# Two chains of the experts' second products as the halves of one PSUM bank

## Chip, cores and metric

One Trainium2 chip, one of its cores. The metric is the device time of one execution, in microseconds, as the median of several runs. TensorE (PE) multiplies and writes PSUM, which has 8 banks of 512 fp32 columns in each of 128 partitions; VectorE (DVE) and ScalarE (ACT) read PSUM; GpSimd (POOL) works from SBUF; SyncE (SP) issues the DMAs.

## What is computed

Linear attention with a random-feature map (4 batches, 8 heads, 576 tokens), whose output is the 2304 x 512 input of a mixture of eight experts. The change lies in the experts' part:

```
def _moe_ref(x, w_gate, w1, w2):
    N, D = x.shape                        # 2304, 512
    E = w_gate.shape[1]                   # 8
    logits = x @ w_gate
    P = np.exp(logits - logits.max())
    for _ in range(8):
        P /= P.sum(1, keepdims=True) + 1e-09
        P /= P.sum(0, keepdims=True) + 1e-09
        P *= N / E
    out = np.zeros((N, D))
    for e in range(E):
        h = np.maximum(x @ w1[e], 0.0)    # w1[e]: 512 x 1024
        out += P[:, e:e + 1] * (h @ w2[e])
    return out
```

## The kernel before

The attention takes the first 180 us or so. Then each of the two products of an expert is done as a 2 x 2 block product by a scheme of seven block products, M1 to M7, in the order 1, 5, 6, 3, 7, 2, 4 (`ORDER`), in which running sums in PSUM serve several blocks of the result. Each factor is split in a high and a low part (`wh`, `wl`; for the left operands `ah`/`al`, `sh`/`sl`, `sh2`/`sl2`, `bh`/`bl`), and each block product is six matmuls: high by high, low by high, high by low, for two halves of the inner dimension.

A unit is an expert and half of its inner columns: 16 units. The 18 row tiles of the tokens go in pairs, a tile t0 of the upper and one, t1, of the lower half of a chunk: nine pairs a unit, and 16 x 9 = 144 steps in all (s = 0 to 143). `second(s, i)` does block product i of the second product of a step, with six matmuls of 256 columns (line 751). Between them the main loop places the pieces of the first product of later steps (`first`, six matmuls of 384 columns each, line 650, into tiles hx and hz of other banks).

The four banks of pool `ps4` hold the sums of `second`. M1, M6, M7, M4 are summed in tile x, one onto the other; M5 and M3 in tile z; M2 alone in tile w. After each of the seven an output operation adds the sum so far, weighted by the gate's column, to one quarter of the pair's result (tiles `out`, 128 x 512 each, one for t0 and one for t1): line 777, a VectorE operation of 256 columns with PSUM and SBUF as sources. For expert 0 (18 steps) the weight comes later and the operation is an addition (line 769) or, for a first value, a ScalarE copy (767). In the last three steps those of M1 and M6 go over ScalarE and GpSimd (774, 775). Since x and z go on summing, M6 waits for M1's operation, M7 for M6's, M4 for M7's and M3 for M5's.

The left operands are made by ScalarE and VectorE: ah and al for M1, sh and sl for M7 and M5 (lines 699 to 713), sh2 and sl2 for M6 and M3, bh and bl for M2 and M4 (lines 725 to 730). bh and bl have one buffer each: those of the next step are written when M4 of this step has read them. GpSimd makes block sums of weights now and then (line 216) and, in the last three steps, sl and sl2.

The order on each engine is not written out by hand in this part: a scheduler orders the instructions by a model of their times and by what depends on what, and gives each tile of a pool a bank that is free then. So a change in one place moves instructions in many.

The lines that set chain and quarter are:

```
key, start = {1: ("x", 1), 6: ("x", 0), 7: ("x", 0), 4: ("x", 0), 5: ("z", 1), 3: ("z", 0), 2: ("w", 1)}[i]
if start:
    acc[key] = bank(key)
pb = acc[key][:, :HD]                     # HD = 256
r, col, init = {
    1: (0, 0, 1), 6: (0, 1, 1), 7: (1, 1, 0), 4: (1, 0, 1), 5: (1, 1, 1), 3: (0, 1, 0), 2: (0, 0, 0),
}[i]                                      # which tile of the pair, which half
```

The two that the change joins are M3, right half of t0, and M2, left half of t0.

Of the kernel before, what the change touches and what calls it, by code (L numbers as in the profile page):

```python
# [22 lines left out]
def moe_attention_kernel(  # L23
# [44 lines left out]
    HD = DM // 2  # L68
# [11 lines left out]
    def bank(name):  # L80
        return ps[0].tile([P, 512], F32, tag="b", name=name)
# [515 lines left out]
    outt = {}  # L597
# [3 lines left out]
    def order(u):  # L601

        return [NCH - 1] + list(range(NCH - 1)) if u == 0 else list(range(NCH))
# [69 lines left out]
    def tiles_of(u, n):  # L673

        c, j = order(u)[n // (CT // 2)], n % (CT // 2)
        return [CT * c + j, CT * c + j + CT // 2]
# [58 lines left out]
    acc = {}  # L735

    def second(s, i):


        u, n = steps[s]  # L740
        key, start = {1: ("x", 1), 6: ("x", 0), 7: ("x", 0), 4: ("x", 0), 5: ("z", 1), 3: ("z", 0), 2: ("w", 1)}[i]
        final = s == len(steps) - 1
        if final and i == 4:

            key, start = "y", 1
        if start:
            acc[key] = bank(key)
        pb = acc[key][:, :HD]
        prods = [(a, b, f) for a, b in ((0, 0), (0, 1), (1, 0)) for f in range(2)]
        for j, (a, b, f) in enumerate(prods):  # L750
            nc.tensor.matmul(  # L751
                pb, lhsT=ops[s][i][a][:, f], rhs=wt[u, 2, i][b][:, f],
                start=bool(start) and j == 0, stop=j == len(prods) - 1, skip_group_check=True,
            )
        e, fb = units[u]
        r, col, init = {
            1: (0, 0, 1), 6: (0, 1, 1), 7: (1, 1, 0), 4: (1, 0, 1), 5: (1, 1, 1), 3: (0, 1, 0), 2: (0, 0, 0),
        }[i]
        pair = tiles_of(u, n)
        t = pair[r]  # L760
        if u == 0 and i == 1:
            for tt in pair:
                outt[tt] = op_.tile([P, DM], F32, name=f"out{tt}")
        o = outt[t][:, col * HD : (col + 1) * HD]
        if e == 0:
            if u == 0 and init:
                nc.scalar.copy(o, pb)  # L767
            else:
                nc.vector.tensor_tensor(o, pb, o, op=ALU.add)
            return  # L770
        p = prob[:, t, e : e + 1]
        if s >= len(steps) - CT // 2 and i in (1, 6):
            sp = op_.tile([P, HD], F32, tag="sp", bufs=2, name="sp")
            nc.scalar.mul(sp, pb, p)
            nc.gpsimd.tensor_tensor(o, sp, o, op=ALU.add)
        else:
            nc.vector.scalar_tensor_tensor(o, in0=pb, scalar=p, in1=o, op0=ALU.mult, op1=ALU.add)  # L777
        if final and i == 7:
            o = outt[t][:, :HD]
            nc.vector.scalar_tensor_tensor(o, in0=pb, scalar=p, in1=o, op0=ALU.mult, op1=ALU.add)  # L780
# [163 lines left out]
    for s, (u, n) in enumerate(steps):  # L944
# [12 lines left out]
        for k, i in enumerate(ORDER):  # L957
            second(s, i)
            if more and (n, k) in W2AT:
                split(u + 1, 2, ORDER[W2AT.index((n, k))])  # L960
            if k < ((5, 5, 4) if s > 2 else (3, 4, 3))[n % 3] and todo:
                pc = todo.pop(0)
                first(*pc)
                j = ORDER.index(pc[2])
                if pc[1] == order(pc[0])[-1] and pc[3] == 1 and pc[0] + 1 < len(units) and j + 1 < len(ORDER):
                    split(pc[0] + 1, 1, ORDER[j + 1])
            if i == 7 and s + 1 < len(steps):
                left_operands_a(s + 1)
            if k in (1, 4):
                next(gate, None)  # L970
# [38 lines left out]
```

## Time and profile before

| | us |
|---|---|
| median of three runs (lowest, highest) | 1613.99 (1610.22, 1614.95) |
| the profiled execution | 1611.28 |
| its span | 1609.4 |
| PE busy | 1574.7 (98%) |
| weight loads of PE (PEld) busy | 1543.1 (96%) |
| DVE busy | 1388.4 (86%) |
| ACT busy | 774.8 (48%) |
| POOL busy | 298.1 (19%) |

An engine's busy time is the union of its instructions' times. A matmul of 256 columns stands in the trace with 0.28 us, but the next starts after half of that, so a pause of PE shorter than the overlap does not show as idle time; its weight loads, which the profile lists apart, show it sooner. A wait is put down to the engine whose signal came last. "x2" on a line of the timeline means two instructions in a row, and its time is that from the first one's start to the last one's end.

### The profile page before, as it was taken

What the parts mean: (1) busy time and instruction counts of PE and PEld (TensorE: products, weight loads), DVE (VectorE), ACT (ScalarE), POOL (GpSimd) and SP (SyncE); (2) the same over time, 40 slices, a digit from 0 to 9 for tenths busy, and PEclk for the clock granted to TensorE, in tenths of its full rate; (3) what the DMA queues carried; (4) which work ended last, traced back from release to release, by engine and by line L of the source; (5) the groups of instructions that cost most, each with busy time, mean ns of one, the idle gap of its engine ahead of it and who ended that gap; (6) DMA issues with size and microseconds to landing.
All of it is one profiled execution on the core that took longest, in us unless ns stands there. A gap on an engine that the chain in (4) does not pass through costs nothing.

```text
span 1609.4 us, 31434 instructions
## 1 busy us (share of the span) xinstructions
PE 1574.7 (98%) x12318; PEld 1543.1 (96%) x12318; DVE 1388.4 (86%) x2721; ACT 774.8 (48%) x1396; POOL 298.1 (19%) x304
## 2 busy tenths in 40 slices
PE   7998899999999999999999999999999999999998
PEld 6877899999999999999999999999999999999997
DVE  5998798999888987989898988889898889889777
ACT  7987565444344444434354444444443444444333
POOL 6664321101021111101021111112010111110003
PEclk9999999999999999999999999999999999999999
DMA  8646865666665665656656665746565566655552
GB/s 205 153 146 240 305 229 203 212 209 208 220 217 192 233 211 171 224 197 215 206 206 213 211 220 181 253 170 223 203 208 210 211 216 212 212 189 198 193 197 79
DMA packets 105314, 329.79 MB, mean 205 GB/s; under 512 B 14800, under 2 KB 43984, under 8 KB 105168
## 3 DMA queue, kind: packets, MB, share of 16 engines
q1 hardware_dynamic: 105168, 327.79, 60.2%
q8 instruction: 98, 1.61, 0.4%
q14 instruction: 48, 0.39, 0.1%
HBM read 306.53 MB, written 21.23 MB: 204 GB/s over the span
## 4 chain that ended last, share of the span: by engine, by line
PE 86%; DVE 10%; ACT 2%; POOL 1%; issue 1%; DMA 0%; SPq 0%; DVEq 0%; ACTq 0%
PE hx L650 24%; PE x L751 23%; PE hz L650 18%; PE z L751 12%; PE w L751 6%; DVE sm L687 2%; DVE out L777 2%; PE pp L389 1%; DVE bl L687 1%; DVE sqs L399 1%; DVE wl L247 1%; POOL sq L353 1%; DVE sl L726 1%; PE tp L374 1%; DVE xs L123 1%
## 5 line engine op out<-in xcount | busy, mean ns | idle before, releaser
L650 PE MATMUL hx<-xs,wh 128*128 128x384 f32 x1536 | 372.2, 336 | 2.7 <-ACT out L767 1.2
L777 DVE SCALAR_TENSOR_TENSOR out<-x,prob,out 128x256 f32<-128x256 f32 x497 | 234.2, 477 | 59.5 <-PE x L751 57.8
L650 PE MATMUL hz<-xs,wh 128*128 128x384 f32 x1152 | 281.7, 337 | 0.0
L650 PEld LDWEIGHTS hx<-xs,wh 128*128 128x128 f32 x1536 | 268.6, 188 | 4.3 <-ACT xs L119 2.0
L216 POOL TENSOR_TENSOR st<-st 128x512 f32<-128x512 f32 x79 | 126.3, 1598 | 702.6 <-DVE wl L247 698.1
L650 PEld LDWEIGHTS hz<-xs,wh 128*128 128x128 f32 x1152 | 203.2, 189 | 0.7 <-ACT xs L119 0.4
L650 PE MATMUL hx<-xs,wl 128*128 128x384 f32 x768 | 198.7, 335 | 0.0
L729 ACT ACTIVATE bh<-hr 128x512 fp32r<-128x512 f32 x144 | 91.2, 633 | 211.6 <-PE x L751 206.9
L777 DVE SCALAR_TENSOR_TENSOR out<-z,prob,out 128x256 f32<-128x256 f32 x252 | 120.3, 478 | 56.5 <-PE z L751 55.9
L725 ACT CAST sh<-sm 128x512 fp32r<-128x512 f32 x144 | 89.6, 622 | 152.7 <-PE z L751 106.1
L246 ACT CAST wh<-st 128x512 fp32r<-128x512 f32 x172 | 102.9, 620 | 104.6 <-PE hx L650 43.9
L650 PE MATMUL hz<-xs,wl 128*128 128x384 f32 x576 | 151.7, 336 | 0.0
L687 DVE SCALAR_TENSOR_TENSOR sm<-hr,sm 128x256 f32<-128x256 f32 x288 | 137.1, 476 | 2.6
L650 PEld LDWEIGHTS hx<-xs,wl 128*128 128x128 f32 x768 | 138.4, 188 | 0.0
L247 DVE TENSOR_TENSOR wl<-st,wh 128x512 fp32r<-128x512 f32 x169 | 121.8, 730 | 12.0 <-ACT wh L246 11.5
L687 DVE SCALAR_TENSOR_TENSOR bl<-hr,bh 128x512 fp32r<-128x512 f32 x144 | 119.5, 830 | 0.1
L751 PE MATMUL x<-wh,sh 128*128 128x256 f32 x576 | 116.9, 283 | 2.6 <-DVE out L777 1.6
L751 PE MATMUL x<-wl,sh 128*128 128x256 f32 x576 | 118.2, 282 | 0.7 <-DVE wl L247 0.7
L751 PE MATMUL x<-wh,sl 128*128 128x256 f32 x576 | 117.2, 282 | 0.0
L751 PE MATMUL z<-wl,sh 128*128 128x256 f32 x576 | 117.2, 281 | 0.0
L751 PE MATMUL z<-wh,sl 128*128 128x256 f32 x576 | 115.3, 282 | 1.7 <-DVE sl L709 1.7
L751 PE MATMUL z<-wh,sh 128*128 128x256 f32 x576 | 116.6, 281 | 0.2 <-DVE out L777 0.2
(161 smaller groups left out, 3410.5 us busy)
## 6 DMA issues: line engine op xcount, KB each, us to landing
xs<-xd SPq DMA_DIRECT2D x329, 768.0 KB, 4.4
st<-in_moe_w_dram SPq DMA_DIRECT2D x64, 512.0 KB, 5.1
xd<-xs SPq DMA_DIRECT2D x21, 768.0 KB, 4.3
k<-in_k_dram SPq DMA_DIRECT2D x8, 512.0 KB, 7.1
v<-in_v_dram SPq DMA_DIRECT2D x8, 512.0 KB, 6.5
q<-in_q_dram SPq DMA_DIRECT2D x8, 512.0 KB, 7.5
out_dram<-out SPq DMA_DIRECT2D x32, 128.0 KB, 1.9
kr<-in_k_dram SPq DMA_DIRECT2D x4, 128.0 KB, 6.6
```

Source lines behind the costliest of these rows:

```text
L123: nc.vector.tensor_tensor(t[:, 1], o, raw(t[:, 0]), op=ALU.subtract)
L216: nc.gpsimd.tensor_tensor(o, a, b, op=op)
L246: nc.scalar.copy(hi, o)
L247: (nc.vector if u > 0 or (w == 2 and i in (1, 6, 7, 4)) else nc.gpsimd).tensor_tensor(lo, o, raw(hi), op=ALU.subtract)
L353: nc.gpsimd.tensor_tensor(s[..., :w], s[..., :w], s[..., w : 2 * w], op=ALU.add)
L374: nc.tensor.transpose(tp[:, i * P : (i + 1) * P], tin[:, o : o + P], ident)
L650: nc.tensor.matmul(pb, lhsT=a[:, k, g * P : (g + 1) * P], rhs=x[:, b, k, :], start=i in (1, 5, 2) and j == 0, stop=j == len(prods) - 1, sk ...
L687: nc.vector.scalar_tensor_tensor(o, in0=a, scalar=0.0, in1=b, op0=ALU.max, op1=op)
L725: nc.scalar.copy(sh, sm)
L729: nc.scalar.activation(bh, a[:, 1:], AF.Relu)
L751: nc.tensor.matmul(pb, lhsT=ops[s][i][a][:, f], rhs=wt[u, 2, i][b][:, f], start=bool(start) and j == 0, stop=j == len(prods) - 1, skip_gro ...
L777: nc.vector.scalar_tensor_tensor(o, in0=pb, scalar=p, in1=o, op0=ALU.mult, op1=ALU.add)
```

## The change

M2 gets no bank of its own. M5 and M3 now go to the right half of tile z (columns 256 to 511) and M2 to its left half, with a start of its own. M3 has no output operation; after M2 one operation of 512 columns takes both halves into t0's whole row. A step so has six output operations in place of seven and uses two banks in place of three. M5's operation, which reads the right half before M3 adds to it, stays.

```
-        key, start = {1: ("x", 1), 6: ("x", 0), 7: ("x", 0), 4: ("x", 0), 5: ("z", 1), 3: ("z", 0), 2: ("w", 1)}[i]
+        key, start = {1: ("x", 1), 6: ("x", 0), 7: ("x", 0), 4: ("x", 0), 5: ("z", 1), 3: ("z", 0), 2: ("z", 0)}[i]
         final = s == len(steps) - 1
...
         if start:
             acc[key] = bank(key)
-        pb = acc[key][:, :HD]
+        pb = acc[key][:, HD:] if i in (5, 3) else acc[key][:, :HD]
+        start = start or i == 2
...
         }[i]
+        if i == 3:
+            return
         pair = tiles_of(u, n)
...
         o = outt[t][:, col * HD : (col + 1) * HD]
+        if i == 2:
+            o, pb = outt[t], acc[key]
```

PE between M4 of step 97 (tile x_14592) and M2 of step 98 (w_14802) in the kernel before:

```order
L751 MATMUL x_14592<-wh_13708,bl_14589 128x256 x2
L751 MATMUL x_14713<-wh_13467,sh2_14703 128x256 x2
L751 MATMUL x_14713<-wl_13468,sh2_14703 128x256 x2
L751 MATMUL x_14713<-wh_13467,sl2_14704 128x256 x2
L751 MATMUL z_14732<-wh_13416,sl_14683 128x256 x2
L751 MATMUL w_14802<-wh_13658,bh_14709 128x256 x2
L751 MATMUL w_14802<-wl_13659,bh_14709 128x256 x2
L751 MATMUL x_14828<-wh_14399,ah_14792 128x256 x2
L751 MATMUL x_14828<-wl_14400,ah_14792 128x256 x2
L751 MATMUL x_14828<-wh_14399,al_14793 128x256 x2
L751 MATMUL w_14802<-wh_13658,bl_14710 128x256 x2
```

The same step now, on PE, from the 11th row behind the last of M4 of step 97 on: M7 (x_14517), M3 and M2 (both z_14536):

```order
L752 MATMUL x_14517<-wh_13411,sh_14487 128x256 x2
L752 MATMUL x_14517<-wl_13412,sh_14487 128x256 x2
L752 MATMUL x_14517<-wh_13411,sl_14488 128x256 x2
L752 MATMUL z_14536<-wh_13361,sh2_14507 128x256 x2
L752 MATMUL z_14536<-wl_13362,sh2_14507 128x256 x2
L752 MATMUL z_14536<-wh_13361,sl2_14508 128x256 x2
L752 MATMUL z_14536<-wh_13480,bh_14513 128x256 x2
L752 MATMUL z_14536<-wl_13481,bh_14513 128x256 x2
L752 MATMUL z_14536<-wh_13480,bl_14514 128x256 x2
```

M2 has moved from ahead of M3 to behind it. M1 of the next step (x_14828 before) and pieces of the first product stand between M4 and these rows now.

PE at step 68, from M5's last products to M3's first (z_11182), in the kernel before:

```order
L751 MATMUL z_11182<-wh_10227,sl_11137 128x256 x2
L751 MATMUL x_11167<-wh_10399,sh_11136 128x256 x2
L751 MATMUL x_11167<-wl_10400,sh_11136 128x256 x2
L751 MATMUL x_11167<-wh_10399,sl_11137 128x256 x2
L751 MATMUL w_11255<-wh_10469,bh_11163 128x256 x2
L751 MATMUL w_11255<-wl_10470,bh_11163 128x256 x2
L751 MATMUL x_11281<-wh_10147,ah_11245 128x256 x2
L751 MATMUL x_11281<-wl_10148,ah_11245 128x256 x2
L751 MATMUL x_11281<-wh_10147,al_11246 128x256 x2
L751 MATMUL z_11182<-wh_10348,sh2_11157 128x256 x2
```

And now (z_11046):

```order
L752 MATMUL z_11046<-wh_10107,sl_11002 128x256 x2
L752 MATMUL x_11031<-wh_10276,sh_11001 128x256 x2
L752 MATMUL x_11031<-wl_10277,sh_11001 128x256 x2
L752 MATMUL x_11031<-wh_10276,sl_11002 128x256 x2
L752 MATMUL z_11046<-wh_10226,sh2_11021 128x256 x2
```

Sixteen products stood between M5 and M3 there, six of M7, four of M2 and six of the next step's M1; M7's six are left.

VectorE's last operations, all on the pair of the last step (t0 is out14, t1 out17), before:

```order
L777 SCALAR_TENSOR_TENSOR out14_3248<-w_19962,prob_79,out14_3248 128x256
L777 SCALAR_TENSOR_TENSOR out14_3248<-z_19930,prob_79,out14_3248 128x256
L777 SCALAR_TENSOR_TENSOR out17_3249<-x_19920,prob_79,out17_3249 128x256
L780 SCALAR_TENSOR_TENSOR out17_3249<-x_19920,prob_79,out17_3249 128x256
L777 SCALAR_TENSOR_TENSOR out17_3249<-y_19970,prob_79,out17_3249 128x256
```

And now:

```order
L782 SCALAR_TENSOR_TENSOR out17_3245<-z_19644,prob_79,out17_3245 128x256
L782 SCALAR_TENSOR_TENSOR out17_3245<-x_19634,prob_79,out17_3245 128x256
L785 SCALAR_TENSOR_TENSOR out17_3245<-x_19634,prob_79,out17_3245 128x256
L782 SCALAR_TENSOR_TENSOR out17_3245<-y_19682,prob_79,out17_3245 128x256
L782 SCALAR_TENSOR_TENSOR out14_3244<-z_19644,prob_79,out14_3244 128x512
```

The three operations that wait for M7 and M4 (x and y) were last and now stand ahead of the merged one, as M3 and M2 are now the last products on PE, where M7's were.

## Rows read from the trace of the kernel before

**Rows 1.** Stretch view; columns: stretch, length, busy PE, PEld, DVE, ACT, POOL, clock, DMA.

```profile
186.00:1580.00 1394.00, 1387.96 (x9808) 1381.60 (x9807) 1214.77 (x2359) 616.00 (x1039) 180.01 (x119) 1.00 0.60 207
1580.00:1610.00 30.00, 21.99 (x169) 20.40 (x168) 21.45 (x42) 9.99 (x19) 12.53 (x12) 0.98 0.29 88
```

**Rows 2.** Waits of PE's weight loads, 186 to 1580: total, times, longest us.

```profile
PEld w L751 <- DVE bl L687: 5.4, 10, 1.5
PEld x L751 <- DVE out L777: 2.2, 3, 1.2
PEld w L751 <- ACT bh L729: 1.1, 2, 0.6
```

**Rows 3.** Timeline at step 98: start, us, engine, what; in brackets the idle time before.

```profile
1168.66 2.84 POOL L216 TENSOR_TENSOR st<-st 128x512 f32<-128x512 f32 x2 [43.72 <-DVE wl L247]
...
1169.06 0.40 PE L751 MATMUL x<-wh,bl 128*128 128x256 f32 x2
...
1170.24 0.40 PE L751 MATMUL w<-wh,bh 128*128 128x256 f32 x2
...
1170.48 0.40 PE L751 MATMUL w<-wl,bh 128*128 128x256 f32 x2
1170.66 1.38 DVE L687 SCALAR_TENSOR_TENSOR bl<-hr,bh 128x512 fp32r<-128x512 f32 x1
...
1172.10 0.30 PEld L751 LDWEIGHTS w<-wh,bl 128*128 128x128 f32 x2 [0.53 <-DVE bl L687]
1172.10 0.50 PE L751 MATMUL w<-wh,bl 128*128 128x256 f32 x2 [0.33 <-DVE bl L687]
```

**Rows 4.** Groups of VectorE: count, busy us, mean ns of one, idle before.

```profile
L687 DVE SCALAR_TENSOR_TENSOR sm<-hr,sm 128x256 f32<-128x256 f32 x288 | 137.1, 476 | 2.6
...
L777 DVE SCALAR_TENSOR_TENSOR out<-z,prob,out 128x256 f32<-128x256 f32 x252 | 120.3, 478 | 56.5 <-PE z L751 55.9 <-POOL out L775 0.2
...
L687 DVE SCALAR_TENSOR_TENSOR sm<-hr,hn 128x512 f32<-128x512 f32 x143 | 101.8, 712 | 3.6 <-ACT hn L665 2.0 <-POOL sl L726 1.1
...
L777 DVE SCALAR_TENSOR_TENSOR out<-w,prob,out 128x256 f32<-128x256 f32 x126 | 60.0, 476 | 24.1 <-PE w L751 23.7
```

**Rows 5.** Stretch view at the start of the experts' part; columns as in rows 1.

```profile
178.00:182.00 4.00, 1.01 (x4) 0.59 (x4) 3.95 (x11) 3.08 (x6) 0.65 (x1) 1.00 1.01 396
182.00:186.00 4.00, 3.96 (x15) 3.96 (x16) 0.95 (x3) 1.20 (x3) 4.00 (x3) 0.57 0.28 117
```

**Rows 6.** Timeline at the start of the experts' part.

```profile
176.59 1.50 DVE L687 SCALAR_TENSOR_TENSOR al<-hr,ah 128x256 fp32r<-128x256 f32 x1
...
182.85 0.84 PE L650 MATMUL hz<-xs,wh 128*128 128x384 f32 x2
...
185.41 0.54 PE L650 MATMUL hz<-xs,wl 128*128 128x384 f32 x2
...
186.49 0.40 PE L751 MATMUL x<-wh,ah 128*128 128x256 f32 x2
```

**Rows 7.** Timeline of the end of the program; SPq is the queue of stores.

```profile
1603.52 0.40 PE L751 MATMUL x<-wh,sl 128*128 128x256 f32 x2
1603.59 0.82 SPq L787 DMA_DIRECT2D out_dram<-out  x2
1603.95 0.48 DVE L777 SCALAR_TENSOR_TENSOR out<-x,prob,out 128x256 f32<-128x256 f32 x1
...
1604.50 2.39 SPq L791 DMA_DIRECT2D out_dram<-out  x4
1604.87 0.48 DVE L777 SCALAR_TENSOR_TENSOR out<-y,prob,out 128x256 f32<-128x256 f32 x1
```

**Rows 8.** Timeline at step 44: an output operation behind bl.

```profile
631.69 0.39 PE L751 MATMUL x<-wh,sl 128*128 128x256 f32 x2
...
633.13 1.76 DVE L687 SCALAR_TENSOR_TENSOR bl<-hr,bh 128x512 fp32r<-128x512 f32 x1
...
634.81 0.47 DVE L777 SCALAR_TENSOR_TENSOR out<-x,prob,out 128x256 f32<-128x256 f32 x1
```

## The prediction

> **What bounds the kernel now.** I read the busy times by stretch first, for the experts' part without its start and end, 186 to 1580 us [rows 1]: of 1394 us TensorE (PE) is busy for 1388, VectorE (DVE) for 1215 and no other engine for half. PE is idle for 6.0 us there, and its weight loads, which show a pause sooner because they run just ahead of the products, for 12.4 us. So whatever the change does to the other engines, some 12 us is all that it can win there, unless it shortens the end or the start. The second view is who ended those pauses of the weight loads [rows 2]: 5.4 us in ten waits of chain M2 (tile w) for its operand bl, 1.1 us in two waits of M2 for bh, and 2.2 us in three waits of x for an output operation. M2 alone has 6.5 of the 12.4 us.
>
> The timeline of one of the ten, at step 98, shows why [rows 3]. GpSimd runs two operations for 2.84 us from 1168.66. Inside that time VectorE's bl of 512 columns takes 1.38 us; the mean of another operation of the same form, sm of 512 columns, is 0.71 [rows 4]. M4 of the step before is through at 1169.46, bl is ready at 1172.04, 2.6 us later, and only 18 products stand between on PE, 2.1 us at the 0.12 us at which products of 256 columns follow each other (two start 0.24 us apart). PE waits 0.53 us. The M2 chain stood there as filler: its four products with bh run at 1170.24 to 1170.9, its last two need bl.
>
> **The change part by part.** *VectorE.* In 126 of the 144 steps two operations of 478 and 476 ns [rows 4] become one of 512 columns, for which no row stands here. From the 256- and 512-column forms of the same operation on SBUF, 476 and 712 ns [rows 4], 256 columns more cost 0.24 us, so I take 0.71 us; the bounds are 0.95 us (no gain) and 0.48 (the second half free). The other 18 steps have additions in their place, for which I take the same saving. That is 144 x 0.24 = 35 us less on VectorE, and I count it as nothing: VectorE is idle for 179 us of the first stretch [rows 1] and PE is the bound. It only shortens queues. If the operation cost as much as the two, nothing of the sum below would change.
>
> *M2 moves behind M3.* M2 now starts a new accumulation in the bank in which M3's was open, and the order has all 144 M2 chains begin behind M3's last product, where before all began ahead of it (by 1.6 us of products or more). This takes M2 further from M4 of the step before, whose end frees the buffer of bh. Counted over the order at 0.12 us a product (0.17 for one of 384 columns), the products between M4's end and M2's first product with bl last under 3.0 us in 36 of 142 steps before, and in 15 now; all ten waits for bl lie in those 36, among them steps 11, 38, 44, 53, 80 and 98. At step 98 it was 2.1 us and is 4.5. The wait of 2.6 us shown above would be covered. A wait also costs the pair after it 0.1 us (0.50 us for a pair in place of 0.40 [rows 3]), so M2's waits are worth 6.5 + 12 x 0.1 = 7.7 us. I keep 15/36 of it: 4.5 us saved. Bounds: 7.7 and 0.
>
> *M3 and M5.* M3 adds to the half that M5's operation reads, as before. But M2's four products, and often M1 of the next step, which stood between M5 and M3, now stand elsewhere. Half of the steps keep 3.8 us of products there, before and after, but the steps with under 1.6 us go from 2 to 18, and eight of the first stretch have 0.7 to 1.1 us (50, 53, 59, 68, 104, 107, 113, 122). In the last rows of the kernel an operation starts 0.03 us after the product that it waits for and takes 0.48 [rows 7]; with one operation ahead of it, as at steps 59 and 68, it ends some 0.7 us after M5. That just fits. I take 8 x 0.06 = 0.5 us lost; bounds 0 and the 18 us of the second rival.
>
> *The merged operation* waits for M2's end, so the right half of row tile t0 is added some 0.7 us of products later than M3's end. Behind it in VectorE's queue stand operand operations of the next steps (sl, sl2 and a wl at step 98); who reads the sum is the same tile of the next unit, some nine steps on, and the store at the end. The x chains gain room: two banks a step in place of three out of four means that a new x or z finds its bank read long before (under 1.6 us of products after the last chain there in 2 cases, 32 before). Their waits for output operations, 2.2 us [rows 2], lie inside chain x, at M6 and M7, and I leave them. Loads on the sync queue change places by one or two, with the same shortest distance for an xs buffer (4.2 us of products, once).
>
> *The start.* After the attention PE is busy for 1.0 of the 4 us from 178 to 182, and in the next 4 us, in which it is busy nearly throughout, the mean granted clock is 0.57, between the two levels of 1.2 and 2.4 GHz [rows 5]. The six products of step 1's M1, which ran at 186.49 after this hole, now stand in front of M5's second pair, and their operand al is ready at 178.09 [rows 6]. That fills 6 x 0.12 = 0.7 us of the hole: 0.7 saved. If it also held the clock, the products of 384 columns from 182.85 on would take 0.54 us a pair in place of 0.84 [rows 6], four pairs, 1.2 us more. Bounds 0 and 1.9.
>
> *The end.* Before, PE's last product ended at 1603.92, three operations followed until 1605.35, and the four last stores were issued from 1604.50 to 1606.89 [rows 7], 2.97 us after PE. Now M3 and M2 are last on PE, one operation of 0.71 us follows, and three stores do, two of 0.41 us (0.82 for two) and one of 0.60 (2.39 for four): 0.04 + 0.71 + 1.42 = 2.17 us. 0.8 saved; bounds 0 and 1.5. In the three steps before, where GpSimd does part of the operands, the order shuffles; PE idles 1.9 us there up to 1603.92 (23.92 us less 21.99 [rows 1]), and I leave that as it is, with 1.9 us either way.
>
> **Sum.** -4.5 + 0.5 - 0.7 - 0.8 = -5.5 us. The profiled execution took 1611.28 us, of which the span is 1609.4: it becomes 1605.8. The median of the runs is 1613.99, 2.7 above that execution; the same 5.5 us off gives 1608.5.
>
> **The rivals.** *The waits move on* (1612.5). VectorE falls behind while GpSimd works, and whichever product needs it next waits. For it: a wait of x stands beside those of w in the same view [rows 2], and 15 steps still have under 3 us. Against it: sm and sl, the next in line, have more room than bl had. Then only start and end are won, 1.5 us: 1612.5, within 0.3%, which is about what a measurement of this kernel can tell from no change.
>
> *M3 waits for M5's operation* (1626, slower). Where the operation is caught behind a stretched bl it is late: in one case a product of x ends at 632.08, bl runs 1.76 us from 633.13, and the output operation behind it is through at 635.28, 3.2 us after the product [rows 8]. If that happened at the eight steps with some 0.95 us of products it would cost 8 x 2.25 = 18 us: 1608.5 - 0.5 + 18 = 1626. It decides the sign from 10 us on, 1.3 us at each. For it: M2 no longer fills there. Against it: GpSimd works at few of the steps, and bl stands behind M5's operation at 59 and 68. Here the Trainium skill speaks against the change: Perfetto Trace Analysis, section Matmuls, wants independent groups of products to rotate through different PSUM banks, so that one is taken out while the next is computed. Held against this kernel it means this rival, with its 1626; the order bears it out at the eight places and nowhere else.
>
> *All waits of M2 go, the start keeps its clock and the end is at its bound* (1603.4): -7.7 + 0.5 - 1.9 - 1.5 = -10.6 us.
>
> **How the numbers follow.** Forecast 0.48, the waits move on 0.30, all waits go 0.12, slower by M3 0.10. Of the forecast's 0.48, 0.40 is faster by more than 0.3% (4.8 us) and 0.08 within. So faster 0.52, same 0.38, slower 0.10. The range goes down to 1601, where every bound of the first stretch, start, end and last steps (7.7, 1.9, 1.5, 1.9) is won, and up to 1615, the first rival with the 2.5 us by which the runs lie around each other (1610.22 to 1614.95); the slower rival is left out.
>
> **What would show it.** In the profile after: waits of z's weight loads for bl and bh of some 3 us where w had 6.5 (none: the third rival; as many on other tiles: the first); the merged operation at 0.71 us; VectorE's busy time down by some 35 us; no wait of z for an output operation over 0.3 us at steps 59 and 68; x<-ah beside mt at 178; from PE's last product to the span's end 0.8 us less than now. PE waits of over 10 us in all on z for output operations would make the forecast wrong in sign.

## The result and the profile after

The changed kernel takes 1597.0 us (1595.8 to 1598.3), the kernel before, run beside it, 1612.8 (1610.2 to 1615.0): a ratio of 0.9904, 95% interval 0.9892 to 0.9916. That is 15.8 us faster, where 5.5 were forecast, and below the range of 1601 to 1615. The profiled execution took 1596.08 us with a span of 1594.3, 15.1 us less than before.

The stretch view of both kernels for the part that is common to them (before first, then after; columns as in [rows 1]):

```profile
186.00:1565.00 1379.00, 1372.96 (x9701) 1366.60 (x9700) 1203.52 (x2337) 611.21 (x1030) 180.01 (x119) 1.00 0.61 209
```

```profile
186.00:1565.00 1379.00, 1378.92 (x9799) 1377.89 (x9798) 1198.26 (x2219) 612.74 (x1037) 177.31 (x119) 1.00 0.61 210
```

In the same 1379 us TensorE (PE) does 98 products more. Its weight loads are idle for 1.1 us in place of 12.4, PE itself for 0.1 in place of 6.0. The waits of the weight loads after, the view that answers [rows 2]:

```profile
PEld z L752 <- DVE out L782: 0.5, 2, 0.2
PEld mb L573 <- PE z L752: 0.3, 1, 0.3
```

No wait for bl or bh is left, and none of x. Step 98, which stood in [rows 3], now reads so in the timeline:

```profile
1154.80 0.39 PE L752 MATMUL x<-wh,bl 128*128 128x256 f32 x2
...
1156.23 0.69 DVE L687 SCALAR_TENSOR_TENSOR bl<-hr,bh 128x512 fp32r<-128x512 f32 x1
...
1156.39 1.67 POOL L216 TENSOR_TENSOR st<-st 128x512 f32<-128x512 f32 x1 [4.11 <-DVE wl L247]
...
1159.56 0.40 PE L752 MATMUL z<-wh,bl 128*128 128x256 f32 x2
```

M4 of the step before is through at 1155.19, bl at 1156.92, and M2 asks for it at 1159.56, 2.6 us later. Two things have changed: M2 stands further back, and bl takes 0.69 us in place of 1.38, since it began 0.16 us ahead of GpSimd's operation and not inside it.

The groups of VectorE after, which answer [rows 4] (count, busy us, mean ns, idle before):

```profile
L726 DVE TENSOR_TENSOR sl<-sm,sh 128x512 fp32r<-128x512 f32 x141 | 114.8, 815 | 39.2 <-ACT sh L725 30.9 <-PE x L752 8.3
L687 DVE SCALAR_TENSOR_TENSOR bl<-hr,bh 128x512 fp32r<-128x512 f32 x144 | 110.0, 764 | 2.4 <-ACT bh L729 2.0 <-PE z L752 0.4
...
L782 DVE SCALAR_TENSOR_TENSOR out<-z,prob,out 128x512 f32<-128x512 f32 x126 | 93.8, 745 | 14.1 <-PE z L752 12.8 <-POOL out L780 0.6
```

The merged operation takes 745 ns where the two took 954. With the 18 additions of expert 0 that is 29 us less, and the durations of all VectorE's operations together fall by 30.8 us (sl grew to 815 ns from 721 and bl shrank to 764 from 830). But VectorE's busy time falls only from 1388.4 to 1373.6 us. Busy time counts a moment in which two records overlap only once, and records of operations in a row overlap by some 0.08 us: in the run with two operations in place of the merged one (the first experiment) the two halves stand in a row, and from the start of the first to the end of the second it is 0.87 us (median of 144), not 0.95:

```profile
710.07 0.48 DVE L773 SCALAR_TENSOR_TENSOR out<-z,prob,out 128x256 f32<-128x256 f32 x1
710.46 0.47 DVE L788 SCALAR_TENSOR_TENSOR out<-z,prob,out 128x256 f32<-128x256 f32 x1
```

The changed kernel has 196 such overlaps fewer, 15.9 us.

The start, which answers [rows 5, 6], and the end, which answers [rows 7]:

```profile
182.00:186.00 4.00, 4.00 (x18) 4.00 (x18) 0.94 (x3) 1.43 (x4) 4.00 (x3) 0.61 0.08 29
```

```profile
175.77 1.50 DVE L687 SCALAR_TENSOR_TENSOR al<-hr,ah 128x256 fp32r<-128x256 f32 x1
...
176.21 0.48 PE L752 MATMUL x<-wh,ah 128*128 128x256 f32 x2
...
181.70 0.82 PE L650 MATMUL hz<-xs,wh 128*128 128x384 f32 x2
...
1588.86 0.39 PE L752 MATMUL z<-wh,bl 128*128 128x256 f32 x2
1589.36 0.75 DVE L782 SCALAR_TENSOR_TENSOR out<-z,prob,out 128x512 f32<-128x512 f32 x1
1590.23 1.04 SPq L792 DMA_DIRECT2D out_dram<-out  x2
1591.32 0.47 SPq L796 DMA_DIRECT2D out_dram<-out  x1
```

The clock fell as before (0.61 mean in 182 to 186, against 0.57), with hz pairs of 0.82 to 0.84 us. From PE's last product (it ends at 1589.25, before at 1603.92) to the end of the span it is 5.05 us, before 5.48.

**Where the 15.1 us went.** For a finer account I take, from the records of all some 10,000 products from 186 us on, the time from one product's start to the next's less the usual 117 ns (256 columns) or 174 ns (384). This excess is 27.2 us before and 14.0 after. So 13.2 us of pauses are gone. Before 186 us PE is 1.5 us ahead, 0.8 of which is there already at al (175.77 against 176.59), in the attention, which the change doesn't touch: that part is luck. The end gives 0.4.

Pauses of over 60 ns in 186 to 1565 us, by the chain that they stand in front of:

| us | M2 | x (M1, M6, M7, M4) | M5, M3 | first products | sum |
|---|---|---|---|---|---|
| before | 7.4 | 5.9 | 0.9 | 0.7 | 14.9 |
| after | 0.0 | 0.3 | 1.1 | 0.4 | 1.9 |

The sums hold 0.1 for a product of the gate. The two columns that I had at -4.5 and at 0 give -7.4 and -5.5.

### The profile page after: what moved, and what is told of

It reads as the page before. It is cut to its first block, busy times and chain, and to the rows that moved or that the text cites. A ratio compares the mean times of both kernels' runs of the same rounds, so it can differ in the third digit from the quotient of the medians.

```text
span 1594.3 us, 31334 instructions
## 1 busy us (share of the span) xinstructions
PE 1565.9 (98%) x12318; PEld 1539.4 (97%) x12318; DVE 1373.6 (86%) x2577; ACT 772.3 (48%) x1396; POOL 296.5 (19%) x304
## 3 DMA queue, kind: packets, MB, share of 16 engines
q8 instruction: 98, 1.61, 0.4%
## 4 chain that ended last, share of the span: by engine, by line
PE 91%; DVE 5%; ACT 2%; POOL 1%; issue 1%; DMA 1%; SPq 0%; DVEq 0%; ACTq 0%
PE x L752 25%; PE hx L650 25%; PE z L752 19%; PE hz L650 19%; PE pp L389 1%; DVE sqs L399 1%; DVE xs L123 1%; POOL sq L353 1%; DVE sm L687 1%; ACT ex L419 0%; PE tp L374 0%; PE qp L485 0%; ACT sq L349 0%; ACT ex L415 0%; DVE xt L528 0%
## 5 line engine op out<-in xcount | busy, mean ns | idle before, releaser
L650 PE MATMUL hz<-xs,wh 128*128 128x384 f32 x1152 | 286.4, 337 | 0.0
L782 DVE SCALAR_TENSOR_TENSOR out<-z,prob,out 128x256 f32<-128x256 f32 x252 | 153.6, 610 | 15.5 <-PE z L752 14.2
L726 DVE TENSOR_TENSOR sl<-sm,sh 128x512 fp32r<-128x512 f32 x141 | 114.8, 815 | 39.2 <-ACT sh L725 30.9
L725 ACT CAST sh<-sm 128x512 fp32r<-128x512 f32 x144 | 89.5, 622 | 106.0 <-PE z L752 83.3
L687 DVE SCALAR_TENSOR_TENSOR sm<-hr,sm 128x256 f32<-128x256 f32 x288 | 132.7, 461 | 3.2
L247 DVE TENSOR_TENSOR wl<-st,wh 128x512 fp32r<-128x512 f32 x169 | 121.8, 729 | 13.7 <-ACT wh L246 13.7
L712 ACT CAST sh<-sm 128x512 fp32r<-128x512 f32 x143 | 89.0, 622 | 65.6 <-PE x L752 62.7
L699 ACT ACTIVATE ah<-hr 128x256 fp32r<-128x256 f32 x144 | 60.2, 418 | 120.7 <-PE x L752 104.6
```

The lines of the kernel that those rows point to most:

```text
L247: (nc.vector if u > 0 or (w == 2 and i in (1, 6, 7, 4)) else nc.gpsimd).tensor_tensor(lo, o, raw(hi), op=ALU.subtract)
L650: nc.tensor.matmul(pb, lhsT=a[:, k, g * P : (g + 1) * P], rhs=x[:, b, k, :], start=i in (1, 5, 2) and j == 0, stop=j == len(prods) - 1, sk ...
L687: nc.vector.scalar_tensor_tensor(o, in0=a, scalar=0.0, in1=b, op0=ALU.max, op1=op)
L699: nc.scalar.activation(ah, a11, AF.Relu)
L712: nc.scalar.copy(sh, sm)
L725: nc.scalar.copy(sh, sm)
```

## Experiments

Theories: *distance* (M2's products with bl stand further behind M4, so bl is there in time); *one operation* (fewer operations, a shorter queue on VectorE); *banks* (two a step in place of three). Later, *luck*: the scheduler happened on a good order. Ratios are to the kernel before, run beside it on the same chip; their 95% intervals stand in brackets.

### Two operations in place of the merged one

```
         if i == 2:
-            o, pb = outt[t], acc[key]
+            o2, pb2 = outt[t][:, HD:], acc[key][:, HD:]
+            if e == 0:
+                nc.vector.tensor_tensor(o2, pb2, o2, op=ALU.add)
+            else:
+                nc.vector.scalar_tensor_tensor(
+                    o2, in0=pb2, scalar=prob[:, t, e : e + 1], in1=o2, op0=ALU.mult, op1=ALU.add
+                )
```

> The changed kernel, but the merged operation is cut in its two halves of 256 columns, both behind M2: two banks a step and M2 behind M3 as in the change, seven output operations as before. Theory of distance (the time was won because M2's products with bl stand further behind M4 of the step before): in the order the products between M4 and M2's first with bl last under 3.0 us in 4 of 143 steps (37 before, 15 after the change), so 1597, within 3 us of the changed kernel, with no wait of z for bl over 0.5 us in all, though VectorE is busy for some 126 x (2 x 0.477 - 0.745) = 26 us more. Theory of the one operation (VectorE's shorter queue won it): most of the 15.8 us come back, 1605 to 1613, and waits of z and x for output operations of 5 us or more. Theory of the banks (two a step in place of three): as the changed kernel.

1598.8 us, 0.9916 [0.9902 to 0.9931]; pauses in the long stretch 1.3 us, none at M2, 0.3 at x. The changed kernel is 1.8 us faster, and the intervals of the two overlap, so the single operation has at most a small part of the gain. That theory falls.

### M2 behind M3, but in a bank of its own

```
+        if i == 2:
+            tc.add_manual_dep(new[0], last["m3"], in_order, reason="M2 behind M3")
```

> The kernel before, M2 in a bank of its own (w) and with an operation of its own, but its first product held behind M3's last in the order. The scheduler then moves M3 forward instead: under 3.0 us stand between M4 and M2's first product with bl in 43 steps (37 before), but never under 2.5 (8 before); and between M5 and M3 there are under 0.9 us in 43 steps (1 before). Theory of distance: bl is still waited for in some of the 43, 3 to 6 us of M2's waits stay, 1606 to 1612. If standing behind M3 were enough by itself: 1597. Theories of the one operation and of the banks: as before, 1611 to 1613. If M3 waits for M5's operation at 0.7 us of products (my second rival), 43 steps with some 0.3 us or more of wait each: 1620 or more.

1631.9 us, 1.0122 [1.0107 to 1.0137]. The waits of the weight loads:

```profile
PEld z L752 <- DVE out L783: 23.0, 40, 0.9
```

M2 hardly pauses (0.6 us), but M3, moved to 0.9 us or less behind M5 in 43 steps, waits for M5's operation in 40: my slower rival, at 0.6 us a step. Place alone does not bring the gain. This kernel and the run before it have seven operations and M2 behind M3 alike; they differ in M2's bank (and in M3's operation, which need not wait for M2 here), by 33 us. They differ in their order as well, so the two do not tell the bank from the order.

### Three banks for the changed kernel

```
-    ps[0] = ctx.enter_context(tc.tile_pool(name="ps4", bufs=4, space=bass.MemoryType.PSUM))
+    ps[0] = ctx.enter_context(tc.tile_pool(name="ps4", bufs=3, space=bass.MemoryType.PSUM))
```

> The changed kernel with three banks in the pool of the second products in place of four. Distance from M4 to M2's bl is long (under 3.0 us in 3 steps), but a new chain finds its bank read under 1.6 us before in 39 steps (2 after the change, 32 before), and M6 to M7 and M5 to M3 are under 1.6 us in 32 and 34. Theory of distance: as the changed kernel, 1597 to 1600. Theory of the banks (what the change won was room between a chain's end and the next use of its bank): x and z wait for output operations again, 5 to 10 us, 1602 to 1610. Theory of the one operation: as the changed kernel.

1673.1 us, 1.0381 [1.0364 to 1.0397], far outside what any theory said.

```profile
PEld z L752 <- DVE out L782: 43.2, 23, 2.4
```

At one place in twelve units M3 waits up to 2.4 us for M5's operation, which at step 44 stands behind a bl and an sm that took 1.61 and 1.48 us beside GpSimd; at another place in eleven units it waits 1.4 us. Behind the long wait of step 44 the granted clock is at its lower level (0.50 from 648.3 to 650.0 us), and pairs of 256 columns take 0.63 us in place of 0.40. The x chains wait for output operations as the theory of the banks had it (6.1 us), but the bulk is again the slower rival.

### M2 ahead of M3 in the shared bank

```
-            second(s, i)
+            second(s, {3: 2, 2: 3}.get(i, i))
...
-        if i == 3:
+        if i == 2:
             return
...
-        if i == 2:
+        if i == 3:
             o, pb = outt[t], acc[key]
```

> The changed kernel with M2 and M3 exchanged: M2 into the left half of tile z ahead of M3, one operation of 512 columns behind M3; two banks, six operations. The order now has under 2.5 us between M4 and M2's first product with bl in 32 steps (3 after the change, 8 before), under 2.0 in 16 (0 and 0). Theory of distance: waits of z for bl and bh come back, at the 16 steps at least 0.3 us each and more where GpSimd works beside: 5 to 12 us, 1602 to 1610. Theories of the one operation and of the banks: as the changed kernel, 1596 to 1598.

1645.5 us, 1.0208 [1.0191 to 1.0225]. M2's first product, which now has to wait for M5's operation on the same tile, pauses 33.6 us in 32 steps, up to 1.95 us. So the run doesn't test distance; it shows that in a shared bank an M2 with a start of its own can only stand behind M3. What it computes differs, too: the right half of t0 lacks M5's products (last section).

### No block sums on GpSimd

```
         def tt(o, a, b, op=ALU.subtract):
+            if u > 0:
+                return
             nc.gpsimd.tensor_tensor(o, a, b, op=op)
```

> The kernel before without GpSimd's block sums of weights from the second unit on (line 216; the products take the plain blocks in place of the sums, so what is computed differs there). The order is as tight as before: under 3.0 us between M4 and M2's products with bl in 41 steps (37), under 2.5 in 15 (8). If the pauses of M2 and of the x chains both come from VectorE operations that run 1.4 to 1.8 us while GpSimd works, in place of 0.7: both go, PE's pauses over 60 ns fall from 18.8 to some 5 us, 1598 to 1603. If tight places pause by themselves: 1608 to 1614, and M2 still waits for bl for 4 us or more.

> The changed kernel without GpSimd's block sums from the second unit on, as in the run beside it. If those sums were the source of the pauses that the change removed, they have nothing left to take here: 1595 to 1598, and the gap between the two kernels shrinks from 15.8 us to 6 or less. If the change won by something else (banks, fewer operations, the order as a whole), the gap stays at 10 us or more.

Kernel before: 1604.0 us, 0.9944 [0.9929 to 0.9959], its pauses down from 14.9 to 7.4 us (M2 3.3, x 2.7). Changed kernel: 1598.7, 0.9907 [0.9892 to 0.9922], pauses 3.3. The sums cost the kernel before about half of its pauses and the changed one nothing; the gap between the two shrinks from 15.8 to 5.3 us. So about half of the pauses of before go with GpSimd's sums (the order is another one, too), not all as I expected (11 us of pauses stayed from 186 us to the end, not 5). Four of those that stayed, of 0.31 us each, are waits of M2 at tight steps (under 3.0 us of products from M4 to M2's first with bl) whose bl took 0.69 us: a tight step alone can make a short pause.

### Two buffers for bh and bl, and its control

```
-        bh = hp_[0].tile([P, 2, 2, P], F32R, tag="bh", bufs=1, name="bh")
-        bl = hp_[0].tile([P, 2, 2, P], F32R, tag="bl", bufs=1, name="bl")
+        bh = hp_[0].tile([P, 2, 2, P], F32R, tag="bh", bufs=2, name="bh")
+        bl = hp_[0].tile([P, 2, 2, P], F32R, tag="bl", bufs=2, name="bl")
...
-        bufs = 7 * w
+        bufs = 7 if w == 1 else 13
```

The control has the last edit alone.

> The kernel before with two buffers each for bh and bl (and 13 in place of 14 for the second weights, for room), so that bl no longer waits for M4 of the step before. M2 keeps its bank, its operation and its place ahead of M3. Theory of distance: M2's waits for bl and bh (8.5 us of pauses over 60 ns at M2) go to under 1 us, those of x stay: 1601 to 1606. Theory of the banks: M2 was only where the pause showed, and x and z pause in its place: 1609 to 1613.

> Control for the run with two buffers: the kernel before with 13 in place of 14 buffers for the second weights and nothing else. The order comes out tighter: under 2.5 us between M4 and M2's products with bl in 23 steps (8 before), and a bank read under 1.6 us before its next use in 48 places (32). Theory of distance: M2's pauses grow from 8.5 to 12 to 20 us, 1614 to 1624. Theory of the banks: those of x grow, M2's stay. If neither matters: 1611 to 1613.

With two buffers M2 doesn't pause at all and x for 1.0 us, but the kernel is slower: 1618.4, 1.0034 [1.0021 to 1.0046]. The new order has hz wait for VectorE:

```profile
PEld hz L650 <- DVE hr L667: 10.4, 12, 0.9
```

The control: 1622.5, 1.0056 [1.0041 to 1.0071], pauses 25.9 us, of which M2 has only 1.5, against 12 to 20 expected, although 46 steps were tight for bl (37 before). The time lies where the theory of distance had it, but not for its reason, and in the form in which I counted it that theory falls. A better count is that of tight steps which meet a stretched bl. From the orders and traces:

| | steps with under 3.0 us from M4 to M2's bl | steps with a bl of over 1.1 us | both |
|---|---|---|---|
| before | 37 | 25 | 11: 20, 26, 38, 44, 53, 74, 80, 89, 98, 119, 125 |
| after | 15 | 14 | 2: 140 and 142 |
| control | 46 | 8 | 1: 11 |

The meeting is not all of it, either. In the kernel before seven of the eleven steps paused at bl (not 20, 26, 74 and 119), and the other three of its ten pauses there, at 11, 83 and 128, had a bl of 0.68 us that began late, behind an sm of 0.95 to 1.40 us. At step 11:

```profile
301.62 1.40 DVE L687 SCALAR_TENSOR_TENSOR sm<-hr,sm 128x256 f32<-128x256 f32 x1
...
302.95 0.68 DVE L687 SCALAR_TENSOR_TENSOR bl<-hr,bh 128x512 fp32r<-128x512 f32 x1
```

What all ten have in common is a tight step and, at it, a VectorE operation stretched beside GpSimd, bl itself or one ahead of it.

And since a small edit of a buffer count moves the time by 10 us, luck is a theory of its own: the next runs shake both kernels.

### Both kernels shaken

Each edit gives a buffer count that PE's arithmetic doesn't need; the scheduler then finds another order. `ah`/`al` or `sh`/`sl` get `bufs=2`, always with the 13 buffers above.

> The changed kernel with 13 in place of 14 buffers for the second weights: the shake that cost the kernel before some 10 us. Theory of room (with two banks and M2 behind M3 the scheduler finds orders without tight places): the order keeps its room (under 3.0 us between M4 and M2's products with bl in 13 steps, a bank read under 1.6 us before its next use once), 1595 to 1600. Theory of luck (the order of the changed kernel happens to miss GpSimd's operations, and any shake loses that): 1603 or more.

> The kernel before, shaken in another way: two buffers each for ah and al (and 13 for the second weights). The order is as tight as that of the kernel before (under 3.0 us between M4 and M2's products with bl in 45 steps, a bank read under 1.6 us before its next use in 38). Theory of room: 1608 to 1622, with pauses of M2 and the x chains of 10 us or more in the long stretch. Theory of luck: anywhere, 1597 as well as 1622.

> The changed kernel with two buffers each for ah and al (and 13 for the second weights), the counterpart of the same edit of the kernel before, which gave 1606.5 with 5.9 us of pauses at the x chains. Theory of the bank: under 1 us of pauses at M2 and x, 1595 to 1604. Theory of luck: 5 us or more of them, 1604 to 1612.

> The kernel before with two buffers each for sh and sl (and 13 for the second weights). M2 keeps its own bank and its own operation, but in this order it stands behind M3 in 103 steps by the scheduler's own choice, under 3.0 us between M4 and its products with bl in 4 steps (37 before), and a bank is read under 1.6 us before its next use in 3 places (32 before). Theory of room: the shared bank isn't needed, 1596 to 1603, with pauses of M2 and the x chains under 3 us in the long stretch. Theory of the banks (three chains a step on four banks pause, however they stand): 1608 or more.

> The changed kernel with the same two buffers for sh and sl. Its long stretch has next to nothing left to win: 1594 to 1599 by the theory of room (room everywhere but at M7 and M5, whose operands no longer wait for the step before); by the theory of luck 1603 or more as likely as not.

> The changed kernel with two buffers each for bh and bl (and 13 for the second weights), the counterpart of the same edit of the kernel before, which gave 1618. Theory of the bank (x chains and M2 have no pauses in any order of the two-bank kernel; what differs is small and elsewhere): M2 and x pause for under 1 us in the long stretch, 1595 to 1604. Theory of luck: pauses of M2 or x of 5 us or more, 1604 to 1612.

| kernel | us | ratio [interval] | pauses: M2 | x | M5, M3 | first | sum |
|---|---|---|---|---|---|---|---|
| before, 13 | 1622.5 | 1.0056 [1.0041 to 1.0071] | 1.5 | 10.4 | 7.9 | 5.9 | 25.9 |
| before, two bl | 1618.4 | 1.0034 [1.0021 to 1.0046] | 0.0 | 1.0 | 1.6 | 16.5 | 19.1 |
| before, two sh | 1613.1 | 1.0003 [0.9994 to 1.0013] | 0.0 | 7.9 | 5.5 | 0.3 | 13.7 |
| before, two ah | 1606.5 | 0.9964 [0.9951 to 0.9977] | 0.4 | 5.9 | 0.9 | 1.9 | 9.3 |
| after, two bl | 1615.5 | 1.0012 [1.0003 to 1.0021] | 0.0 | 3.0 | 16.2 | 1.3 | 20.5 |
| after, 13 | 1603.6 | 0.9945 [0.9928 to 0.9961] | 0.2 | 0.3 | 2.5 | 5.1 | 8.2 |
| after, two sh | 1601.5 | 0.9934 [0.9919 to 0.9949] | 0.0 | 0.5 | 0.8 | 0.3 | 1.6 |
| after, two ah | 1599.0 | 0.9913 [0.9894 to 0.9932] | 0.0 | 0.4 | 0.3 | 2.4 | 3.1 |

(A little of a sum is the gate's.) Three readings. With one bank for M5, M3 and M2, M2 pauses for 0.2 us at most and x for under 0.5 us in all orders but one; with three banks x pauses for 5.9 us or more in all but one. The mean ratio of the six two-bank orders (these four, the changed kernel, the one with two operations) is 0.9937, that of the five three-bank orders (the kernel before and its four; the kernels that force or forbid something are left out) 1.0011: by these few, some 12 of the 15.8 us belong to the shared bank and some 4 to the order found. With the same edit the kernel with the shared bank is the faster one in all five pairs (the two unedited kernels are one of them), by 0.0022 (two bl) to 0.0111 (13) of the time of the kernel before. And the spread within each kind is 16 to 19 us, as much as the change: of the shaken two-bank orders one came out where I had put luck, 1603.6 with 5.1 us of pauses at the first products, and one beyond it, 1615.5. The one at 1601.5 lost little in the long stretch (1.6 us) and the rest at the start and the end. The kernel before with two sh, whose order is as roomy in M2 and in banks as the changed one, stayed at 1613; its waits went to M6 for sl2 and to M3. So my theory of room, by which it should have taken 1603 or less, falls as well.

### The slower rival once more, with and without GpSimd

The changed kernel with two buffers for bl is the one two-bank order that gains nothing. Its timeline at step 45:

```profile
643.85 1.29 POOL L216 TENSOR_TENSOR st<-st 128x512 f32<-128x512 f32 x1 [2.43 <-DVE wl L247]
...
644.09 1.33 DVE L687 SCALAR_TENSOR_TENSOR sm<-hr,sm 128x256 f32<-128x256 f32 x1
...
647.33 0.47 DVE L782 SCALAR_TENSOR_TENSOR out<-z,prob,out 128x256 f32<-128x256 f32 x1
...
647.85 0.50 PE L752 MATMUL z<-wh,sh 128*128 128x256 f32 x2 [1.19 <-DVE out L782]
```

An sm of 256 columns takes 1.33 us beside GpSimd (the mean is 476 ns in [rows 4]), VectorE's queue is late from there on, and M5's operation, 3.2 us further on, comes too late for M3, which pauses 1.35 us, at the same place of eleven units. The order had over 2.6 us of products between M5 and M3 there.

> The changed kernel with two buffers for bh and bl (1615.5, with 16 us of pauses at M3), without GpSimd's block sums from the second unit on (the products take the plain blocks in place of the sums, so what is computed differs there). In its order M3 follows M5 after 0.7 us of products in 16 steps (2 with the sums), so that M3's wait for M5's operation has every chance to show. If pauses need GpSimd beside VectorE: those of M3 fall from 16 to 4 us or less (16 x 0.2), 1598 to 1603. If VectorE's queue or the tight places make them by themselves: 8 us or more at M3, 1606 to 1616.

Without the sums: 1601.8 us, 0.9939 [0.9923 to 0.9956], pauses 2.4 us, of M3 1.5 in place of 16.0, though M3 now follows M5 after 0.7 us in 16 steps. The tight places cost 0.1 us each. In this order a long pause takes a VectorE queue that GpSimd has made late.

### The last three steps

```
-        return nc.gpsimd if s >= len(steps) - CT // 2 else nc.vector
+        return nc.vector
...
-        if s >= len(steps) - CT // 2 and i in (1, 6):
+        if False:
```

The second of the two runs has the first edit alone.

> The changed kernel without GpSimd in the last three steps: sl and sl2 are made by VectorE, and the outputs of M1 and M6 go straight from PSUM by VectorE as in the other steps. The order up to the last three steps is the same. In those steps VectorE's operations on SBUF took 0.96 to 1.75 us beside GpSimd in place of 0.41 to 0.69. If GpSimd costs VectorE there more than it takes off it: the last 30 us shrink by 1 to 3 us, 1594 to 1596. If VectorE becomes the bound of the last steps (six operations more in each): 1 to 5 us slower, 1598 to 1602.

> Half of the run beside it: sl and sl2 of the last three steps by VectorE, the outputs of M1 and M6 still over ScalarE and GpSimd. GpSimd works some 2 us a step in place of 4.5, VectorE does two operations of 0.69 us more a step. If the stretching by GpSimd is the cost: 0.5 to 2.5 us less than the changed kernel, 1594.5 to 1596.5; if VectorE's queue is: 1 to 3 us more.

Without GpSimd: 1597.4, 0.9903 [0.9887 to 0.9920]. With sl and sl2 on VectorE alone: 1596.0, 0.9894 [0.9877 to 0.9910]; the pauses behind 1565 us fall from 4.8 to 2.5. That is the fastest kernel here, but it can't be told from the changed one (0.9904).

## Why the prediction was wrong

**What bounds the kernel: right.** PE, with some 12 us of pauses to win. I saw 12.4 us in the weight loads, and 11.3 of them went; counted as pauses it is 13.0 of 14.9.

**M2's waits, -4.5: the step that failed by size.** "I keep 15/36 of it" takes the share of tight steps for the share of waits. The ten waits for bl did all stand at tight steps (36 in my count then, 37 in the later one), but only at such as met an operation stretched beside GpSimd, bl or an sm ahead of it. After, no tight step of the long stretch has a stretched bl, none paused at M2, and all of it went: 7.4 us. The control with 46 tight steps and 1.5 us of pauses shows that the count of tight steps says little. My bound of 7.7 was right, and I took too little of it.

**The x chains, 0: the step that failed outright.** "Their waits for output operations lie inside chain x, and I leave them." Behind the three waits of 2.2 us [rows 2] stood more: six single pauses of 2.9 us together (the longest 1.16 us at M7 of step 26, 0.58 at M6 of 47, 0.50 at M4 of 17), and 30 of about 0.1 us each, many right behind a longer one. All but 0.3 us went, and even the lower end of my range had nothing for them. They were waits of the same kind as M2's: at the longest three the output operation stood behind an operation stretched beside GpSimd, an sm of 1.51 us, an sl of 0.99 and a wl of 1.79. I had named a reason to look again (a bank read under 1.6 us before its next use in 2 cases in place of 32) and put no number on it. By itself it is small, since only M1 takes a new bank, and pauses in front of M1 make 0.8 of the 5.9 us. Nor do the cases tell the pauses of x in other orders: with two sh there are 3, and x paused for 7.9 us; with two bl there are 7, and it paused for 1.0.

**M3 behind M5, +0.5: right.** Pauses of M3 rose by 0.6 us; the longest are 0.20 us, at steps 68 and 122, of the eight that I named. M1 filled the hole at the start as I had it (176.21, beside mt), worth 0.7 us, and the clock still fell: right. The end: -0.4 in place of -0.8; from PE's last product to the last store's issue it took 2.54 us, not 2.17, two stores 1.04 us and not 0.82. The last three steps: +0.9, within the 1.9.

**VectorE, -35 us and worth nothing: half right.** The operation took 745 ns and not 710, and 29 us of durations went; the busy time fell by 14.8, since two operations in a row overlap, which my sum of 478 and 476 ns left out. It was worth next to nothing, as the run with two operations shows.

**The rivals.** "All waits of M2 go" came nearest in its mechanism, but its 1603.4 left x out, too. "The waits move on" did not happen to this order, but to the same kernel with two buffers for bl. "M3 waits for M5's operation" is real: 27 us of pauses in the second run, 47 in the third, 16 in the one with two bl. It had the right mechanism and the wrong condition; it isn't the eight tight places alone that decide, but also where VectorE's queue is late. The rule of the Trainium skill that stood beside it (Perfetto Trace Analysis, section Matmuls: independent groups rotate through different banks) is another matter, since M3 goes on with M5's sum and waits for its operation in the second run, too, where M2 has a bank of its own. What the rule is about shows in the run with M2 ahead of M3: there M2 waits 33.6 us for the operation that reads the other group of its bank. For the changed kernel it did not come true: with M2 behind M3 the two groups in one bank were faster, 0.9904.

What stays open: why orders with the shared bank pause less. Not the number of operations, not M2's place by itself, not the tight steps that I can count. The changed kernel's order on PE was not run with a third bank a step, which would have told the order from the bank. So the cause is shown as far as the pauses that went and the late queue in front of them; that the shared bank makes such orders rests on five pairs.

## What to carry to other kernels

Where a scheduler sets the order, a change of resources gives a new order, and the pauses of the old one are no guide to which stay: ask of every pause what had to meet for it, and take the range from none of them left to all moved on. Shake both kernels by an idle buffer or two before a gain of 1% is put down to the change; here the shakes alone spread over 16 to 19 us, and the pairs with the same edit say more than any single one. Look first for the engine that makes a queue late (GpSimd beside VectorE) and only then for the tight places in which it shows.

## What the runs showed of the hardware

A start in one half of a PSUM bank touches the sum that is open in the other half. In the run with M2 ahead of M3, M2's start falls between M5 and M3, in other columns of the same bank, and the output is off by 0.803 of its norm; leaving M5's products out of the right half of t0 in the reference's computation gives 0.80 as well. The Trainium skill states it (PSUM — Partial Sum Buffer, The four PSUM rules: of two groups open in one bank the second one's start makes the first one's next product overwrite its sum), and the run agrees. It is why an M2 with a start of its own has to stand behind M3. An M2 without one was not run.

GpSimd's block sums and VectorE's bl take turns by whole instructions, and who starts first isn't held up. In the traces before and after bl began ahead of GpSimd's operation in five cases and took 0.68 to 0.69 us in all of them; begun inside one it took up to 1.81. At step 98 bl began 0.16 us ahead of GpSimd's operation and took its 0.69 us, and GpSimd's took 1.67 in place of the 1.29 seen elsewhere. In [rows 3] it was the other way round, with bl at 1.38. The Trainium skill has this, for VectorE operations with two inputs in SBUF, as an exclusive lock that the first one holds for its whole instruction (SBUF — State Buffer, SBUF: two separate sides); both traces agree.

The operation of 512 columns on PSUM takes 745 ns, two of 256 columns together 954, but 0.87 us when they stand in a row: joining them saves 0.21 us of durations and some 0.12 us of VectorE's time.
